# Moving a row store and a load behind the last shared V piece, and a new layout for the other branch's scratch

## The chip, the cores and the metric

The kernel runs on one core of a Trainium2 chip. The metric is the device time of one execution in microseconds (us); less is better. Times of single instructions come from one profiled execution.

## The reference

Two branches are computed from the same x and mixed by a gate. One is a recurrent attention over segments of 32 rows, in which 8 rows of each segment's output are carried to the next; the other is a gated feed-forward. S = 2048, Dm = 640, 32 heads of 192, Df = 1536.

```python
def _A_ref(x, mem0, Wq, Wk, Wv, Wo, seg_len):
    ...
    mem = mem0                                     # 8 rows
    for s in range(n_seg):                         # 64 segments
        xs = x[:, s * seg_len:(s + 1) * seg_len, :].copy()
        h = jnp.concatenate([mem, xs], axis=1)     # 40 rows
        q = jnp.einsum('btd,dhe->bhte', h, Wq)     # k and v alike
        ...
        p = _softmax(scores, axis=-1)
        o = jnp.einsum('bhqk,bhke->bhqe', p, v)
        o = jnp.einsum('bhte,hed->btd', o, Wo)
        mem = o[:, :M, :].copy()
        outs.append(o[:, M:, :])
...
g = _sigmoid((x * gate_w).sum(-1, keepdims=True))
a = _A_ref(x, A_mem0, A_Wq, A_Wk, A_Wv, A_Wo, A_seg_len)
b = _B_ref(x, B_w_gate, B_w_up, B_w_down)          # gelu(x wg) * (x wu), times w_down
return g * a + (1 - g) * b
```

## The kernel before

The program is one list of operations that a small scheduler of the kernel's own (`_Sched`) cuts into five streams, one for each engine. It does not reorder: within an engine the order is that in which the Python code adds them, and semaphores are put in where regions of memory overlap. A DMA is an operation of the engine that issues it. SP (SyncE) issues nearly all of them; in the first stage a few stand in the stream of ACT (ScalarE), since the variable `AUXQ` is "act" there and "sp" from line 909 on.

First stage, the feed-forward branch: four blocks of 512 rows. `ffn_gu` makes gate, up and their product, `ffn_down` the down projection in four steps of 128 rows. In each step PE (TensorE) writes two PSUM banks; ACT (L872) and then DVE (VectorE, L875) copy them to one of four row buffers (`brow`), and a DMA on ACT's queue (L878) stores the 128 rows to the scratch tensor `b_scr` in DRAM. A step's PSUM banks are used again two steps later, its row buffer a block later. Meanwhile SP loads attention weights that fit.

Second stage: 64 segments, one after the other, each written out as a list of items in `PROGS` (four lists, used in turn; segment s has list s % 4). An item ("g", n, k) is one step k = 0 to 4 of a group of projections; group 0 makes Q and K of the first eight heads' "octet", group 1 V of the first octet with Q and K of the second, group 6 V of the last octet. "tq", "tk", "sc", "ex", "pt", "pv" are transposes, scores, softmax and the product with V; ("wo", i, h) is the output projection. The wo items, the addition of the two partial sums and the transpose of the new memory rows (L1463) end a segment, and the next segment's first group needs those rows.

The weights do not all fit on the chip. Thirteen pieces of Q, K and V (384 KB each, one of them cut to 144 KB) and three of Wo (480 KB) share their place with a partner: the place holds the piece of the first octet or that of the last one. Even segments go through the octets upwards, odd ones downwards, so each place is swapped once in a segment: when a step has used the first octet's piece, `swap_loads` puts the load of its partner (L645, for the short one L642) on SP's queue, and it is needed later in the same segment. The five V pieces are swapped after the steps of group 1 and used in the steps of group 6; the K and Q pieces are swapped before them, those of Wo after ("wo", 0, 0) and ("wo", 0, 1).

Around them SP has small transfers, in the order of the code: `out_store` (L1015) writes the finished rows of the segment before from the buffer `bz` to the output; `x_load` (L751) fetches the next segment's rows into `xs`, from where POOL (GpSimd) copies them (`x_copy`, L799) when group 6 is done; `bz_load` (L1006) fetches the feed-forward rows of this segment into `bz`, after group 6, when the row store has landed; POOL scales them (L1042) and DVE mixes them with the attention rows (L1044). The carried rows of each four segments are mixed apart, with `bzl_load` (L1011) and `outl_store` (L1020). `bz` has 128 partitions: partition 32 j + t holds columns 160 j to 160 j + 159 of row t. Further loads and stores on SP bring projections of the left-over rows made ahead (`stg_load` L994, `left_store` L945, L950, `xl_load` L755).

In `segment`, the row store and the x load are added when item ("g", 1, 4) has been issued to PE, and the swap loads of that item, with the fifth V piece, behind them.

Of the kernel before, what the change touches and what calls it, by code (L numbers as in the profile page):

```python
# [6 lines left out]
BF = mybir.dt.bfloat16  # L7
# [224 lines left out]
def _build(nc, A_x, A_mem0, A_Wq, A_Wk, A_Wv, A_Wo, seg_len, w_gate, w_up, w_down,  # L232
           gate_w, out, opts=None):
    opts = dict(opts or {})
    Bsz, S, Dm = A_x.shape
# [3 lines left out]
    L = int(seg_len)  # L239
# [3 lines left out]
    DJ = Dm // 4  # L243
# [4 lines left out]
    NSEG = S // L  # L248
# [3 lines left out]
    XA = L - M  # L252
# [14 lines left out]
    S_ = _Sched(nc)  # L267
# [2 lines left out]

    x2 = A_x[0]
    out2 = out[0]
    b_scr = nc.dram_tensor("ffn_b_scratch", (S, Dm), BF, kind="Internal").ap()
    x_scr = nc.dram_tensor("x_scratch", (NSEG, 128, KT * XA), BF, kind="Internal").ap()
    xl_scr = nc.dram_tensor("left_x_scratch", (NG, 128, KT * 32), BF, kind="Internal").ap()
    g_scr = nc.dram_tensor("gate_scratch", (S,), F32, kind="Internal").ap()
# [431 lines left out]
    def rows(ap, g):  # L708
        v = ap[128 * g:128 * g + 128, :].rearrange("(s t) d -> s t d", t=L)
        return v[:, 0:XA, :], v[:, XA:L, :]  # L710
# [146 lines left out]
    def ffn_down(blk):  # L857
        n1 = min(Dm, 512)
        for a in range(FA):
            xb = 3 + 2 * (a % 2)  # L860
            yb = xb + 1
            fns = []
            for f in range(FT):
                fns.append(lambda e, f=f, a=a, xb=xb: e.matmul(ps[:, xb, 0:n1], hT_sb[:, f, a * 128:(a + 1) * 128], wd_sb[:, f, 0:n1],
                                                               start=(f == 0), stop=(f == FT - 1)))
                if Dm > 512:
                    fns.append(lambda e, f=f, a=a, yb=yb: e.matmul(ps[:, yb, 0:Dm - 512], hT_sb[:, f, a * 128:(a + 1) * 128], wd_sb[:, f, 512:Dm],
                                                                   start=(f == 0), stop=(f == FT - 1)))
            wr = [r_ps[xb]] + ([r_ps[yb]] if Dm > 512 else [])
            S_.add("pe", fns, reads=[r_wd] + r_hT, writes=wr, name="ffn down %d %d" % (blk, a))  # L870
            bs = a % NBR
            S_.add("act", lambda e, bs=bs, xb=xb: e.activation(out=brow[bs][:, 0:n1], in_=ps[:, xb, 0:n1], func=ACTF.Copy),  # L872
                   reads=[r_ps[xb]], writes=[r_brow[bs]], name="ffn b evac")
            if Dm > 512:
                S_.add("dve", lambda e, bs=bs, yb=yb: e.tensor_copy(out=brow[bs][:, 512:Dm], in_=ps[:, yb, 0:Dm - 512]),  # L875
                       reads=[r_ps[yb]], writes=[r_brow[bs]], name="ffn b evac2")
            row0 = blk * FB + a * 128
            S_.add(AUXQ, lambda e, bs=bs, row0=row0: e.dma_start(b_scr[row0:row0 + 128, :], brow[bs]),  # L878
                   reads=[r_brow[bs]], writes=[Rg("dr", row0, row0 + 128)], dma_sem="bw%d" % bs, watch=True,
                   name="b store %d" % row0)  # L880

    ffn_transposes(0)
    x_stage(0)
# [119 lines left out]
               name="Kl s%d i%d" % (s, i))  # L1003

    def bz_load(s):
        S_.add(AUXQ, lambda e: e.dma_start(bz, b_scr[L * s:L * s + L, :].rearrange("t (j n) -> j t n", j=4)),  # L1006
               reads=[Rg("dr", 128 * (s // 4), 128 * (s // 4) + 128)], writes=[r_bz], dma_sem="bz", name="bz load s%d" % s)

    def bzl_load(g):
        for j in range(4):  # L1010
            S_.add(AUXQ, lambda e, j=j: e.dma_start(bzl[32 * j:32 * j + 32], rows(b_scr, g)[1][:, :, DJ * j:DJ * (j + 1)]),  # L1011
                   reads=[Rg("dr", 128 * g, 128 * g + 128)], writes=[r_bzlj[j]], dma_sem="bzl%d" % j, name="bzl load g%d" % g)

    def out_store(s):
# [360 lines left out]
    def segment(s):  # L1375
        g, q = s // 4, s % 4
        n_wo, nqkv = n_wos[q], nqkvs[q]
        held = []
        post = []
        for n, item in enumerate(PROGS[q]):  # L1380
            kind, i = item[0], item[1]
            if kind == "g":
                if item[1:] == (0, 0):
                    left_fill(s, 0)
                    if s:
                        S_.add("pool", lambda e: e.memset(pl_sb[0:104, :, M * ((q + 3) % 4):M * ((q + 3) % 4) + M], 0.0),
                               writes=[r_p], name="pl zero s%d" % s)
                proj(s, item)
                ki = [j for m, j in GROUPS[i] if m == 1 and item[2] == KT - 1]
                kind, i = ("k", ki[0]) if ki else ("", 0)  # L1390
                if kind == "k" and i == 1:
                    if s > 0:
                        out_store(s - 1)
                    if s + 1 < NSEG:
                        x_load(s + 1)
            elif kind == "tq":
                row_transp(s, 0, i)
            elif kind == "tk":
                row_transp(s, 1, i)
            elif kind == "sc":  # L1400
                scores(s, i)
                if i == 0 and q == 0 and g > 0:
                    left_sums(g - 1)
            elif kind == "ex":
                softmax(s, i)
            elif kind == "pt":
                p_transp(s, i)
            elif kind == "pv":
                pv_oct(s, i)
                if i == 0 and q == 3 and g + 1 < NG:  # L1410
                    xl_load(g + 1, XLx, r_XLx, "xlx")
            elif kind == "lf":
                if i == q and unit(s, item[2]):
                    if item[3] == 0:
                        for m in range(2):
                            lb[item[2], m] = misc_bank(s)
                    for m in range(2):
                        LBK[m] = lb[item[2], m]
                    left_mm(*unit(s, item[2]), item[3], unit_piece)
            elif kind == "vb":  # L1420
                if q == 3 and g + 1 < NG:
                    if i == 0:
                        lb["v"] = misc_bank(s)
                    vl_mm(s + 1, i)
            elif kind == "le":
                if i == q and unit(s, item[2]):
                    if n > n_wo:
                        post.append(item[2:] + (n,))
                    else:
                        left_evac(s, *item[2:], n)  # L1430
            else:
                held = wo_part(s, item)
                if i == 2 and item[2] == 0 and q == 0 and g > 0:
                    outl_store(g - 1)
                if q == 3 and item != last_wo:
                    wo_left(s, held)
            if item == gate_at[q]:
                gate_now(s)
            swap_loads(s, item)
            if item == ("wo", 2, 1) and s + 1 < NSEG:  # L1440
                stg_load(s + 1, 0)
            if s == 0 and item == ("g", 0, KT - 1):
                load_residents(3, lambda key: key[0] < 3 and on_tmp(key))
            if s == 0 and item == late_at:
                load_residents(3, lambda key: key[0] == 3)
            if n == nqkv:
                bz_load(s)
                if q == 2:
                    bzl_load(g)
                if q == 3 and g + 2 < NG:  # L1450
                    xl_load(g + 2, XL, r_XL, "xl0")
            if n == nqkv and s + 1 < NSEG:
                x_copy(s + 1)
            if n == nqkv and q == 3:
                scale_left(g)
        kv = [x.rearrange("p (c k) -> p c k", k=KT) for x in (Zt, ps[:, OB2, SC:512], zsum)]
        for i in range(2):
            ka, kb = KA[i], KA[i + 1]
            S_.add("dve", lambda e, ka=ka, kb=kb: e.tensor_tensor(
                out=kv[0][:, :, ka:kb], in0=kv[1][:, :, ka:kb], in1=kv[2][:, :, ka:kb], op=ALU.add),  # L1460
                reads=[r_ps[OB2], r_zp], writes=[r_Z[i]] + ([r_PT] if i == 0 else []), name="Z%s evac s%d" % ("a" if i == 0 else "", s))
            if s + 1 < NSEG:
                S_.add("dve", lambda e, ka=ka, kb=kb: e.transpose(  # L1463
                    out=XB4[:, :, ka:kb, XA:L].rearrange("p g k i -> p k g i"), in_=kv[0][:, :, ka:kb].rearrange("p c k -> p k c")),
                    reads=[r_Z[i]], writes=[r_Hm[i], r_Qm, r_Ql], name="Tm%d s%d" % (i, s))
        mix(s)
        if "v" in lb:
            vl_evac(s + 1, octet(s + 1, 0), lb.pop("v"), "act")
        for i in post:
            left_evac(s, *i)  # L1470
        if q == 3:
            wo_left(s, held)
            if s + 1 == NSEG:
                left_sums(g)
        if s + 1 < NSEG:
            stg_load(s + 1, 1)
# [84 lines left out]
```

## Time and profile before

| | us |
|---|---|
| time, median of 3 runs | 1728.7 (1721.29 to 1739.44) |
| the profiled execution | 1730.04 |
| its span on the core | 1728.2 |
| busy: PE / PEld / DVE / ACT / POOL | 1595.5 / 830.6 / 961.2 / 798.0 / 413.9 |
| first stage, about | 185 |
| DMA: HBM read / written | 458.64 MB / 21.11 MB |

PE is the matrix engine's matmuls, PEld its weight loads. "Lnnn" is a line of the kernel. A row of the timeline has the start in us from the span's start, the length, the engine and the instruction; SPq and ACTq are issues of DMAs, which take issue time on that engine's queue and land later. In square brackets stands the idle time of the engine ahead of the row and what ended it. A row of the view of waits has who waited for whom, the total in us, the number of waits and the longest.

### The profile page before, as it was taken

How to read it: one execution, taken by the hardware profiler on the slowest of the kernel's cores; microseconds unless marked ns; L12 is line 12 of the kernel's file. 1: busy time of each engine (PE TensorE's matmuls, PEld its weight loads, DVE VectorE, ACT ScalarE, POOL GpSimd, SP SyncE). 2: the span in 40 equal slices, each digit the busy share in tenths (PEclk: the TensorE clock that was granted, in tenths of full speed). 3: DMA queues.
4: the chain of work that ended last, by engine and by line, in shares of the span. 5: the costliest groups of instructions: out<-in, count | busy, mean ns of one | idle time of the engine just before them, and what ended most of it. 6: DMA issues, size and time to landing. Idle time of an engine off the chain costs nothing. (4 is left out here: it accounts for less than half of the span.)

```text
span 1728.2 us, 80542 instructions
## 1 busy us (share of the span) xinstructions
PE 1595.5 (92%) x39162; PEld 830.6 (48%) x31501; DVE 961.2 (56%) x2939; ACT 798.0 (46%) x1899; POOL 413.9 (24%) x1098
## 2 busy tenths in 40 slices
PE   9999899999898999999998999999898999999887
PEld 4554345444544545444554545454445445454444
DVE  2222655656565565656565656656555655556554
ACT  3222444444444454545454454545444544445444
POOL 1100122222222222222222222222222222222222
PEclk9999999999999999999999999999999999999999
DMA  9914888878888788888888888888878877879876
GB/s 317 322 54 136 305 288 303 289 259 287 302 285 272 280 301 307 294 285 290 286 301 295 279 293 294 300 307 297 282 265 294 303 283 279 296 283 318 276 272 246
DMA packets 273761, 485.00 MB, mean 281 GB/s; under 512 B 107624, under 2 KB 142720, under 8 KB 273408
## 3 DMA queue, kind: packets, MB, share of 16 engines
q1 hardware_dynamic: 270424, 476.80, 78.8%
q8 instruction: 276, 4.52, 1.0%
q10 hardware_dynamic: 2984, 3.05, 0.5%
q14 instruction: 77, 0.63, 0.1%
HBM read 458.64 MB, written 21.11 MB: 278 GB/s over the span
## 5 line engine op out<-in xcount | busy, mean ns | idle before, releaser
L1115 PE MATMUL ps<-arena 128*32 128x384 bf16 x9940 | 719.5, 328 | 40.5 <-DVE arena L1463 12.0
L226 PE MATMUL ps<-arena 128*32 128x384 bf16 x7680 | 584.3, 326 | 9.3 <-DVE arena L1284 3.5
L1115 PEld LDWEIGHTS ps<-arena 128*32 128x32 bf16 x9940 | 257.9, 96 | 421.4 <-issue 269.1
L1149 DVE STREAM_TRANSPOSE arena<-arena 128x384 bf16<-128x384 bf16 x512 | 275.2, 560 | 116.2 <-ACT arena L1135 115.9
L1135 ACT ACTIVATE arena<-ps 128x384 bf16<-128x384 f32 x512 | 237.0, 490 | 181.0 <-PE ps L1115 155.9
L1275 PE MATMUL ps<-arena 128*32 128x320 bf16 x6144 | 283.5, 302 | 11.5 <-issue 11.4
L1265 POOL COPY arena<-arena 128x96 bf16<-128x96 bf16 x256 | 163.3, 638 | 480.1 <-ACT arena L1257 431.9
L1257 ACT ACTIVATE arena<-ps 128x480 bf16<-128x480 f32 (+1 forms) x256 | 137.3, 537 | 183.2 <-PE ps L1248 180.0
L1275 PEld LDWEIGHTS ps<-arena 128*32 128x32 bf16 x6144 | 174.8, 107 | 63.9 <-issue 18.0
L1000 POOL COPY arena<-arena 128x96 bf16<-128x96 bf16 x256 | 69.4, 271 | 502.6 <-PE ps L1169 402.3
L1138 ACT ACTIVATE arena<-ps 128x384 bf16<-128x384 f32 x256 | 125.0, 488 | 125.0 <-PE ps L1115 122.7
L1181 DVE TENSOR_REDUCE arena<-ps 104x4 f32<-104x160 f32 x256 | 82.9, 324 | 167.0 <-PE ps L1169 165.5
L1231 ACT ACTIVATE arena<-ps 128x448 bf16<-128x448 f32 x192 | 104.7, 545 | 72.1 <-PE ps L1218 72.1
L1246 PE MATMUL ps<-arena 128*64 128x160 bf16 x1536 | 119.6, 243 | 16.3 <-ACT arena L1138 11.8
L1195 DVE TENSOR_REDUCE arena<-ps 104x4 f32<-104x160 f32 x256 | 81.1, 317 | 95.6 <-ACT ps L1193 93.5
L1246 PEld LDWEIGHTS ps<-arena 128*64 128x64 bf16 x1536 | 79.9, 109 | 85.6 <-ACT arena L1231 27.3
L1193 ACT ACTIVATE ps<-ps 104x160 f32<-104x160 f32 x256 | 74.3, 290 | 96.9 <-DVE ps L1183 95.5
L931 PE MATMUL ps<-arena 128*32 128x384 bf16 x1280 | 108.4, 327 | 1.9 <-issue 1.7
L1248 PE MATMUL ps<-arena 128*64 128x64 bf16 x1536 | 103.3, 193 | 3.0 <-issue 3.0
L938 DVE STREAM_TRANSPOSE arena<-arena 128x384 bf16<-128x384 bf16 x128 | 73.8, 576 | 55.4 <-ACT arena L936 49.7
L1183 DVE TENSOR_TENSOR ps<-ps,arena 104x160 f32<-104x160 f32 x256 | 85.1, 332 | 8.8
L1298 PE MATMUL ps<-arena 128*32 128x160 bf16 x3072 | 73.4, 233 | 17.4 <-ACT arena L1033 9.1
(84 smaller groups left out, 1813.5 us busy)
## 6 DMA issues: line engine op xcount, KB each, us to landing
arena<-in_A_Wk_dram SPq DMA_DIRECT2D x335, 384.0 KB, 6.6
arena<-in_A_Wv_dram SPq DMA_DIRECT2D x335, 384.0 KB, 8.4
arena<-in_A_Wo_dram SPq DMA_DIRECT2D x205, 480.0 KB, 6.0
arena<-in_A_Wq_dram SPq DMA_DIRECT2D x146, 384.0 KB, 5.7
arena<-left_qk_scratch SPq DMA_DIRECT2D x126, 96.0 KB, 2.4
left_qk_scratch<-arena SPq DMA_DIRECT2D x49, 192.0 KB, 3.5
arena<-in_A_Wq_dram SPq DMA_DIRECT2D x63, 144.0 KB, 3.7
left_qk_scratch<-arena SPq DMA_DIRECT2D x30, 96.0 KB, 3.0
```

The lines of the kernel that those rows point to most:

```text
L226: return e.add_instruction(mybir.InstMatmult(name=nm, start_tensor_calc=like["start"], stop_tensor_calc=stop, tile_size=(128, 32), tile_po ...
L931: fns.append(lambda e, outp=outp, rhs=rhs, j=j: e.matmul(outp, lhs, rhs, start=(k == 0), stop=(k == KT - 1), tile_position=(0, 32 * j)))
L1115: fns.append(lambda e, outp=outp, rhs=rhs, j=j: e.matmul(outp, lhs, rhs, start=(k == 0), stop=(k == KT - 1), tile_position=(0, 32 * j)))
L1135: S_.add("act", lambda e, m=m, bk=bk: e.activation(out=rows_sb[m], in_=ps[:, bk, 0:384], func=ACTF.Copy), reads=[r_ps[bk]], writes=[r_rows ...
L1138: S_.add("act", lambda e, i=i, bk=bk: e.activation(out=v_sb[i % NVB].rearrange("p (c n) -> p c n", c=3), in_=ps[:, bk, 0:384].rearrange("p ...
L1149: S_.add("dve", lambda e: e.transpose(out=dst[:, :, 0:L], in_=rows_sb[m].rearrange("p (c r) -> p c r", r=L)), reads=[r_rows[m]], writes=[r ...
L1231: S_.add("act", lambda e: e.activation(out=PT, in_=ps[:, bank, 0:PTW + 128], func=ACTF.Copy), reads=[r_ps[bank]], writes=[r_PT], name="pT ...
L1246: return [lambda e: e.matmul(full, v[:, e0:e0 + 64], PTm[:, i], start=True, stop=False, tile_position=(0, 64 * i), skip_group_check=True), ...
L1248: lambda e: e.matmul(part, vl[:, e0:e0 + 64], PTl[:, i], start=False, stop=True, tile_position=(0, 64 * i), skip_group_check=True)]
L1257: S_.add("act", lambda e: e.activation(out=apx(u[:, 0, 0, :], [[R, na], [3 * R, 4], [1, R]]), in_=ps[:, A, 0:na * W].rearrange("p (c t r) ...
L1265: S_.add("pool", lambda e: e.tensor_copy(out=uTl[:, q, :, 12 * oc:12 * oc + 12].rearrange("p i (t c) -> p t c i", c=3), in_=u[:, :, :, L:R ...
L1275: fns.append(lambda e, i=i, t=t, j=j, gv=gv: e.matmul(ps[32 * j:32 * j + 32, bank, 0:2 * DJ].rearrange("p (h n) -> p h n", h=2), lhs2[i], ...
```

## The change

Two edits. In `segment`, a flag is set at item ("g", 1, 4), and the row store and the x load are added behind `swap_loads` of that item instead of ahead of it, so that the load of the fifth V piece comes first. And the scratch `b_scr` gets the shape (segment, quarter of the columns, row, 160 columns): the 128 rows of a store are four segments, so each store becomes four DMAs of 32 rows with a semaphore of its own, and the load of `bz` reads one contiguous block. The left-over load reads its 8 rows of four segments from the new shape.

```diff
-    b_scr = nc.dram_tensor("ffn_b_scratch", (S, Dm), BF, kind="Internal").ap()
+    b_scr = nc.dram_tensor("ffn_b_scratch", (NSEG, 4, L, DJ), BF, kind="Internal").ap()
@@ ffn_down
-            S_.add(AUXQ, lambda e, bs=bs, row0=row0: e.dma_start(b_scr[row0:row0 + 128, :], brow[bs]),
-                   reads=[r_brow[bs]], writes=[Rg("dr", row0, row0 + 128)], dma_sem="bw%d" % bs, watch=True,
-                   name="b store %d" % row0)
+            for i in range(4):
+                S_.add(AUXQ, lambda e, bs=bs, row0=row0, i=i: e.dma_start(
+                    b_scr[row0 // L + i].rearrange("j t n -> t j n"), brow[bs][L * i:L * i + L].rearrange("t (j n) -> t j n", j=4)),
+                    reads=[r_brow[bs]], writes=[Rg("dr", row0 + L * i, row0 + L * i + L)], dma_sem="bw%d%d" % (bs, i), watch=True,
+                    name="b store %d" % row0)
@@ bz_load
-        S_.add(AUXQ, lambda e: e.dma_start(bz, b_scr[L * s:L * s + L, :].rearrange("t (j n) -> j t n", j=4)),
+        S_.add(AUXQ, lambda e: e.dma_start(bz, b_scr[s].rearrange("j t n -> (j t) n")),
@@ bzl_load
-            S_.add(AUXQ, lambda e, j=j: e.dma_start(bzl[32 * j:32 * j + 32], rows(b_scr, g)[1][:, :, DJ * j:DJ * (j + 1)]),
+            S_.add(AUXQ, lambda e, j=j: e.dma_start(bzl[32 * j:32 * j + 32], b_scr[4 * g:4 * g + 4, j, XA:L, :]),
@@ segment
+        turn = False
         for n, item in enumerate(PROGS[q]):
...
                 if kind == "k" and i == 1:
-                    if s > 0:
-                        out_store(s - 1)
-                    if s + 1 < NSEG:
-                        x_load(s + 1)
+                    turn = True
...
             swap_loads(s, item)
+            if turn:
+                if s > 0:
+                    out_store(s - 1)
+                if s + 1 < NSEG:
+                    x_load(s + 1)
+                turn = False
```

## Prediction, made before the changed kernel was run

> **What bounds the kernel now.** I read the page's busy lines first, then the windows by stage, then who waited for whom, and last the timeline of SP (SyncE, which issues nearly all DMAs) in one segment.
>
> ```profile
> span 1728.2 us, 80542 instructions
> PE 1595.5 (92%) x39162; PEld 830.6 (48%) x31501; DVE 961.2 (56%) x2939; ACT 798.0 (46%) x1899; POOL 413.9 (24%) x1098
> ...
> q10 hardware_dynamic: 2984, 3.05, 0.5%
> ```
>
> The windows by stage have the length, the busy time of PE, PEld, DVE, ACT and POOL with counts, the clock, the DMA engines' share and GB/s. The first two rows are the feed-forward branch, the third is the 64 segments.
>
> ```profile
> 0.00:90.00 90.00, 86.39 (x537) 43.64 (x547) 23.17 (x40) 24.90 (x39) 11.40 (x30) 1.00 0.94 313
> 90.00:185.00 95.00, 91.25 (x748) 43.36 (x634) 29.09 (x62) 26.92 (x47) 5.85 (x16) 0.99 0.38 117
> 185.00:1728.00 1543.00, 1417.89 (x37886) 743.61 (x30328) 908.95 (x2837) 746.16 (x1813) 396.61 (x1052) 1.00 0.82 289
> ```
>
> TensorE is busy 1417.9 of 1543 us of the segments, at full clock: a segment is 1543/64 = 24.1 us long, of which PE idles 1.95 us. The DMA engines are busy 82% of that stage. Two things can set the end here: PE's own work, and the stream of weight pieces that are swapped in each segment. From the view of waits I take the rows of PE and PEld that name a DMA, and one of POOL (total us, times, longest):
>
> ```profile
> PEld ps L1115 <- DMA arena<-in_A_Wv_dram: 15.4, 30, 2.2
> ...
> PE ps L1115 <- DMA arena<-in_A_Wk_dram: 11.1, 22, 2.0
> ...
> PEld ps L1298 <- DMA arena<-in_A_Wo_dram: 8.1, 15, 1.0
> POOL arena L1042 <- DMA arena<-ffn_b_scratch: 7.5, 15, 1.4
> PE ps L1115 <- DMA arena<-in_A_Wv_dram: 6.4, 10, 1.7
> ...
> PE ps L1298 <- DMA arena<-in_A_Wo_dram: 4.9, 12, 0.8
> ```
>
> PE stands still for V pieces 6.4 us, for Wo pieces 4.9 us and for K pieces 11.1 us in the whole run. The PEld rows (weight loads, partly under running matmuls) are the upper ends. K pieces are requested and land before anything that is moved, so theirs stay. That leaves 6.4 us at stake for V, at the most 15.4.
>
> **The move of the row store and the x load.** This is SP in one segment of the second program (start, length of the issue):
>
> ```profile
> 796.69 1.63 SPq L645 DMA_DIRECT2D arena<-in_A_Wv_dram  x3
> 798.36 0.56 SPq L1015 DMA_DIRECT2D out_dram<-arena  x1
> 798.96 0.60 SPq L751 DMA_DIRECT2D arena<-x_scratch  x1
> 799.61 0.51 SPq L645 DMA_DIRECT2D arena<-in_A_Wv_dram  x1
> 803.86 1.28 SPq L645 DMA_DIRECT2D arena<-in_A_Wo_dram  x3
> 805.66 0.55 SPq L1006 DMA_DIRECT2D arena<-ffn_b_scratch  x1
> 810.79 0.37 SPq L945 DMA_DIRECT2D left_qk_scratch<-arena  x1
> ```
>
> The fifth shared V piece (k = 4; V4 below) is issued at 799.61, 0.05 us after the x load's issue ends: SP doesn't wait for PE there, so V4 simply moves up to 798.36, by 1.25 us. The row store (L1015) moves back by V4's 0.51 and the x load likewise. What they were moved past is V4 alone; nothing else on SP is between.
>
> Whether V4 also lands 1.25 us earlier, the landings of V2, V3, V4 and of the x load tell (each answer is for that one issue: start in us, and us from it to landing):
>
> ```profile
> L645 SPq DMA_DIRECT2D arena<-in_A_Wv_dram x1: 562/562/562, 797.3 to 797.3; - x1
> ...
> DMA to landing us min/median/max: 8.2/8.2/8.2
> ```
>
> ```profile
> L645 SPq DMA_DIRECT2D arena<-in_A_Wv_dram x1: 442/442/442, 797.9 to 797.9; - x1
> ...
> DMA to landing us min/median/max: 8.5/8.5/8.5
> ```
>
> ```profile
> L645 SPq DMA_DIRECT2D arena<-in_A_Wv_dram x1: 512/512/512, 799.6 to 799.6; - x1
> ...
> DMA to landing us min/median/max: 7.9/7.9/7.9
> ```
>
> ```profile
> L751 SPq DMA_DIRECT2D arena<-x_scratch x1: 602/602/602, 799.0 to 799.0; - x1
> ...
> DMA to landing us min/median/max: 7.6/7.6/7.6
> ```
>
> V2 lands at 805.5, V3 at 806.4, the x load at 806.6, V4 at 807.5. V3 follows V2 by 0.9 us and V4 follows V3 by 1.1: the transfers stand in a queue that takes each about 8 us, and the two small ones between them cost 0.2 us of it. So V4 lands 0.2 us earlier, not 1.25 (ends: 0, if another transfer sets its last share, and 1.25, if the issue did); I take 0.2, from the spacing. Does PE wait for V4? The timeline of PE and POOL around it:
>
> ```profile
> 807.55 0.22 PE L1213 MATMUL ps<-arena 104*32 104x80 bf16 x4 [0.30 <-DVE arena L1199]
> ...
> 807.72 0.34 PE L1115 MATMUL ps<-arena 128*32 128x384 bf16 x4
> ...
> 808.14 0.29 POOL L799 COPY arena<-arena 128x120 bf16<-128x120 bf16 x1 [0.36 <-PE ps L1115]
> ...
> 811.65 0.39 PE L1298 MATMUL ps<-arena 128*32 128x160 bf16 x12 [0.74 <-DMA arena<-in_A_Wo_dram]
> ```
>
> V4's matmuls run at 807.72, and PE's idle 0.30 us ahead of them was ended by DVE (the softmax), not by V4, which had landed at 807.5. An earlier V4 brings nothing in this segment. The ten PE waits for V are shared by five pieces, of which V4 comes last and with most time. I put the gain at 0.5 us: ten waits, one in four for V4, 0.2 us each. Ends: 0 and 6.4 us. The last Wo piece is what PE waits for at 811.65; ahead of it in the queue stand the same bytes as before, in another order, so its 0.74 us stay.
>
> What comes later: the x load lands behind V4, so at about 807.5 instead of 806.6. Its reader, POOL's copy L799, starts at 808.14 and was released by PE, which had finished V4; 0.6 us of slack are left, and behind that PE's next segment starts only after 811.65. Without that cover it would cost at most the 0.9 us per segment by which the x load is later. I take 0.
>
> The row store lands later too, and SP's next load of bz (L1006) waits for it. The view of waits of SP:
>
> ```profile
> SPq L1006 <- DMA out_dram<-arena: 10.5, 15, 2.1
> ```
>
> In the segment shown, L1006 is issued at 805.66 and could slip to 807.5 at most. Queued behind it on SP is the store at 810.79, which waits for DVE; from 806.21 on SP has 4.6 us free. So the 1.8 us vanish in it: 0 (if the cover were gone: first rival on the slow side, below).
>
> **The new scratch layout.** The load of bz reads one contiguous 40 KB block instead of four strided ones; its 128 runs of 320 B stay. It may be issued 0.1 us faster and land earlier; who gains is POOL L1042 (7.5 us of waits), then the mix on DVE. No PE row names either, so 0; the left-over loads (L1011) keep their form. The stores of the feed-forward branch change more: 16 DMAs of 128 rows of 1280 B become 64 of 32 rows of 4 x 320 B, on ACT's queue. The timeline of ACT in that stage, and issue times of stores by form (ns min/median/max):
>
> ```profile
> 120.94 0.60 ACT L872 ACTIVATE arena<-ps 128x512 bf16<-128x512 f32 x1 [1.49 <-PE ps L867]
> 121.97 0.35 ACTq L878 DMA_DIRECT2D ffn_b_scratch<-arena  x1
> 124.20 0.60 ACT L872 ACTIVATE arena<-ps 128x512 bf16<-128x512 f32 x1 [2.66 <-PE ps L867]
> ...
> 133.96 0.60 ACT L852 ACTIVATE arena<-ps 128x512 bf16<-128x512 f32 x1 [1.31 <-PE ps L846]
> ```
>
> ```profile
> L878 ACTq DMA_DIRECT2D ffn_b_scratch<-arena x16: 326/349/353, 40.8 to 171.7; - x16
> ```
>
> ```profile
> L945 SPq DMA_DIRECT2D left_qk_scratch<-arena x49: 372/380/1337, 175.3 to 1578.3; - x49
> ```
>
> ```profile
> L1020 ACTq DMA_DIRECT2D out_dram<-arena x2: 728/740/753, 1724.8 to 1725.6; - x2
> ```
>
> One step of 128 rows takes 124.20 - 120.94 = 3.26 us. ACT uses 0.60 for its copy, 0.43 waiting for DVE's, 0.35 for the store: 1.38. Three more stores at 0.38 (L945, the nearest form: four runs from each partition) are 1.14 more: 2.52 of 3.26, under PE's matmuls. At 0.74 (L1020, the dearest store that ACT issues) the step takes 0.60 + 0.43 + 2.96 = 3.99, 0.73 too long, 16 times: 11.7 us if all of it shows. Lower end 0. After the fourth step of a block the next thing on ACT is the gelu, which has 1.31 us idle ahead of it, more than 1.14. After the last block ACT's first copy of the left-over rows starts up to 1.1 us late, and a DVE chain behind it holds PE once:
>
> ```profile
> PE ps L226 <- DVE ps L786: 2.2, 1, 2.2
> ```
>
> That wait can grow by 0 to 1.1 us; ACT's idle time between those copies takes most of it, so +0.3. Bytes stay the same; queue q10 gets 48 x 128 = 6144 packets more, all small.
>
> The Trainium skill speaks against this part: "DMA: Bandwidth & Descriptors", Specifications, wants at least 512 B per transfer for full rate, since shorter ones are read, changed and written back. By it the stores of 320 B would cost about twice; as an estimate from that page's rule that is q10's 0.5% of the span again, some 9 us of DMA time, half of it in the first 90 us, where the engines are busy 94%. No run here shows it yet for stores of this size beside larger ones, and the sum goes without it.
>
> **The sum.** The profiled execution took 1730.0 us (span 1728.2 and 1.8 around it): 1730.0 - 0.5 + 0.3 = 1729.8. It lies 1.3 above the median of the three runs, 1728.7, so on that scale I predict 1728.5.
>
> **Rivals.**
> (a) The stream is relieved more than I think: with the row store off V4's way and the bz load no longer strided, transfers stop lagging and PE's waits for V and Wo go, both in PEld rows, 15.4 + 8.1 = 23.5 us: 1705. For it: these waits come in a stage whose DMA engines are 82% busy. Against: V2 and V3 are ahead of the moved transfers, and the bytes ahead of Wo are the same. The Trainium skill, "DMA: Bandwidth & Descriptors", Why a DMA increments its semaphore by 16, has a rule that bears on it: a DMA uses as many of the 16 engines as divide its slowest dimension, so bz's four strided blocks would sit on 4 engines and the contiguous load on 16; no row here tells the engines apart.
> (b) Slower: the row store's later landing holds SP at L1006 past its cover, and the K requests of the next segment, in order behind it, go out late. Programs 1 and 3, where L1006 follows the row store most closely, are 32 segments; at 1.1 us each (V4's spacing) that is 35 us: 1764. For it: 15 such waits exist already. Against: 4.6 us of idle SP behind it. It decides once the delay exceeds those 4.6 us.
> (c) ACT becomes the bound in the down projection, at 0.74 us a store: 1728.5 + 11.7 = 1740. For it: that row is ACT's own. Against: it is a store of 8 rows in four blocks, another form.
> (d) V4 can't be issued earlier since PE has not released its slot: then the order on SP changes and V4's landing doesn't: 1729. Against: the zero wait at 799.61.
>
> **How the numbers follow.** My forecast 0.78, (a) 0.06, (b) 0.06, (c) 0.07, (d) 0.03. A measurement of this kernel can tell about 1%, 17 us, from no change. (a) is faster by more, (b) slower by more, the rest within: 0.06, 0.88, 0.06. The range: 1728.5 less the 6.4 us of V and some of the runs' own spread (1721 to 1739) gives 1719; plus (c) 1740. It leaves out (a) and (b).
>
> **What would show it.** Right: in the profile after, SP's L751 and L1015 stand behind the fifth V load; V4's landing moves by some tenths of a us; the PE waits for Wv stay between 4 and 7 us and PE's busy time stays; the ACT stores take under 0.45 us each and the first two windows keep their PE time. Wrong: Wv and Wo waits of PE near zero (a), longer waits of L1006 together with more Wk waits (b), PE idle in the down projection (c).

## The result and the profile after

The changed kernel takes 1733.95 us (median of 22 runs, 1725.45 to 1744.3), the kernel before 1725.88 in the runs beside it (22 runs, 1718.03 to 1739.44): ratio 1.0047, 95% interval 1.0032 to 1.0062. It is 8 us slower. The profiled execution took 1733.92 us.

The page of the changed kernel, and its windows by stage (columns as before):

```profile
span 1732.2 us, 80614 instructions
...
PE 1602.0 (92%) x39162; PEld 833.9 (48%) x31501; DVE 962.1 (56%) x2939; ACT 798.5 (46%) x1899; POOL 415.8 (24%) x1098
...
q10 hardware_dynamic: 9896, 3.05, 0.8%
```

```profile
0.00:90.00 90.00, 86.18 (x536) 43.28 (x546) 23.07 (x40) 24.81 (x39) 11.44 (x30) 1.00 0.95 312
90.00:185.00 95.00, 89.93 (x724) 42.75 (x612) 28.97 (x62) 27.05 (x47) 5.88 (x16) 1.00 0.41 118
185.00:1732.00 1547.00, 1425.84 (x37912) 747.87 (x30344) 910.08 (x2837) 746.61 (x1813) 398.51 (x1052) 0.99 0.82 288
```

The first stage is as long as before (its last copy at L872 starts at 170.9 us, at 170.8 in before); what is lost is lost in the segments, with PE 7.9 us longer busy at a granted clock of 0.99 instead of 1.00. The waits of PE for weight pieces (total us, times, longest), then two waits of other engines:

```profile
PE ps L1117 <- DMA arena<-in_A_Wk_dram: 11.5, 21, 1.5
...
PE ps L1300 <- DMA arena<-in_A_Wo_dram: 3.9, 10, 0.8
...
PE ps L1117 <- DMA arena<-in_A_Wv_dram: 2.7, 9, 0.6
PE ps L226 <- DMA arena<-in_A_Wq_dram: 2.5, 3, 1.4
```

```profile
SPq L1008 <- DMA out_dram<-arena: 31.3, 25, 2.6
...
POOL arena L1044 <- DMA arena<-ffn_b_scratch: 9.9, 15, 1.0
```

V waits fell from 6.4 to 2.7 us. New is a row for Wq, 2.5 us where the view of before has 0.2. The wait of the bz load for the row store grew from 10.5 to 31.3 us. The issues of the two lines that changed their form (ns min/median/max), the bz load before and after, then the store after:

```profile
L1006 SPq DMA_DIRECT2D arena<-ffn_b_scratch x64: 537/548/632, 200.5 to 1714.4; - x64
```

```profile
L1008 SPq DMA_DIRECT2D arena<-ffn_b_scratch x64: 326/431/1842, 200.6 to 1718.0; - x64
```

```profile
L879 ACTq DMA_DIRECT2D ffn_b_scratch<-arena x64: 309/453/1570, 40.5 to 173.5; - x64
```

The bz load's median is 0.12 us shorter, but some issues take over three times as long as before. What follows one of them on SP, in the changed kernel, at the end of a segment with s % 4 = 2 ("program 2" from here; start and length in us):

```profile
727.74 1.84 SPq L1008 DMA_DIRECT2D arena<-ffn_b_scratch  x1
729.63 2.92 SPq L1013 DMA_DIRECT2D arena<-ffn_b_scratch  x4
732.59 0.44 SPq L952 DMA_DIRECT2D left_qk_scratch<-arena  x1
733.14 1.48 SPq L996 DMA_DIRECT2D arena<-left_qk_scratch  x1
734.67 0.43 SPq L645 DMA_DIRECT2D arena<-in_A_Wk_dram  x1
735.14 0.43 SPq L642 DMA_DIRECT2D arena<-in_A_Wq_dram  x1
```

The same place in the kernel before, in another segment of that program:

```profile
1117.79 0.56 SPq L1006 DMA_DIRECT2D arena<-ffn_b_scratch  x1
1118.39 2.59 SPq L1011 DMA_DIRECT2D arena<-ffn_b_scratch  x4
1121.03 0.45 SPq L950 DMA_DIRECT2D left_qk_scratch<-arena  x1
1121.58 0.45 SPq L994 DMA_DIRECT2D arena<-left_qk_scratch  x1
1122.07 0.44 SPq L645 DMA_DIRECT2D arena<-in_A_Wk_dram  x1
```

SP has no idle time between the bz load and the next segment's first K piece: every row begins 0.04 to 0.11 us after the end of the one ahead. So what the bz load takes longer, K is requested later. The two rows of DVE that end these segments and the next ones, after and before:

```profile
730.82 0.29 DVE L1469 STREAM_TRANSPOSE arena<-arena 128x96 bf16<-128x96 bf16 x1
...
758.08 0.30 DVE L1469 STREAM_TRANSPOSE arena<-arena 128x96 bf16<-128x96 bf16 x1
```

```profile
1120.91 0.29 DVE L1463 STREAM_TRANSPOSE arena<-arena 128x96 bf16<-128x96 bf16 x1
...
1145.31 0.30 DVE L1463 STREAM_TRANSPOSE arena<-arena 128x96 bf16<-128x96 bf16 x1
```

In before K is requested 0.87 us after the segment's start and the segment takes 24.4 us; after the long issue it is 3.56 us (the stage load L996, with 1.48, has its part in it) and 27.3 us. PE in that long segment (in brackets the idle time ahead and what ended it), and the windows around the last of the waits:

```profile
741.42 0.33 PE L226 MATMUL ps<-arena 128*32 128x384 bf16 x4 [0.88 <-DMA arena<-in_A_Wq_dram]
...
743.35 0.35 PE L1117 MATMUL ps<-arena 128*32 128x384 bf16 x4 [0.59 <-DMA arena<-in_A_Wk_dram]
745.01 0.35 PE L1117 MATMUL ps<-arena 128*32 128x384 bf16 x4 [1.32 <-DMA arena<-in_A_Wk_dram]
...
745.94 0.49 PE L1117 MATMUL ps<-arena 128*32 128x384 bf16 x4 [0.16 <-DMA arena<-in_A_Wk_dram]
```

```profile
742.00:745.80 3.80, 1.87 (x46) 0.99 (x42) 1.91 (x7) 1.00 (x3) 0.54 (x2) 1.00 1.03 399
745.90:749.40 3.50, 3.46 (x66) 2.23 (x70) 0.78 (x2) 1.53 (x3) 0.64 (x1) 0.52 1.04 373
749.60:753.00 3.40, 3.40 (x100) 2.68 (x96) 1.19 (x5) 0.76 (x2) 0.65 (x1) 1.00 0.95 347
```

PE waits 2.95 us for Q and K pieces, and then a second price comes: for 3.5 us the granted clock is 0.52, so that 3.5 x 0.48 = 1.7 us more are lost. Such stretches at half clock are what brings the stage's mean from 1.00 to 0.99: seven begin in this trace between the first segment and the last, two in that of before. But only two of the seven, and one of the two, begin in a segment that follows program 2, so this pair of traces alone doesn't tie the clock to the bz load.

### The profile page after: what moved, and what is told of

Read it like the earlier page. It is cut to its first block, busy times and chain, and to the rows that moved or that the text cites. A ratio compares the mean times of both kernels' runs of the same rounds, so it can differ in the third digit from the quotient of the medians.

```text
span 1732.2 us, 80614 instructions
## 1 busy us (share of the span) xinstructions
PE 1602.0 (92%) x39162; PEld 833.9 (48%) x31501; DVE 962.1 (56%) x2939; ACT 798.5 (46%) x1899; POOL 415.8 (24%) x1098
## 4 chain that ended last, share of the span: by engine, by line
PE 72%; DMA 13%; DVE 7%; ACT 3%; issue 3%; ACTq 1%; SPq 0%; POOLq 0%; DVEq 0%; POOL 0%
PE ps L1117 21%; PE ps L226 15%; PE ps L1277 10%; DMA arena<-in_A_Wk_dram 7%; PE ps L1248 4%; DMA arena<-in_A_Wo_dram 3%; PE ps L1300 3%; PE ps L849 3%; PE ps L846 3%; PE ps L1171 2%; DMA arena<-in_A_Wv_dram 2%; PE ps L933 2%; PE ps L1158 2%; PE ps L864 2%; PE ps L1166 1%
```

## The experiments

Each ratio is to the kernel before, run beside it, with its 95% interval in brackets. "128-row form" is the bz load from 128 equal rows, as in the changed kernel; "four-block form" is that of before, four blocks of 32 rows that can't be joined.

**First: which part.** e1 has the order change alone, e2 the new layout alone, e3 the layout with a padding row that brings the four-block form back:

```diff
# e3
-    b_scr = nc.dram_tensor("ffn_b_scratch", (NSEG, 4, L, DJ), BF, kind="Internal").ap()
+    b_scr = nc.dram_tensor("ffn_b_scratch", (NSEG, 4, L + 1, DJ), BF, kind="Internal").ap()[:, :, 0:L, :]
-        ... e.dma_start(bz, b_scr[s].rearrange("j t n -> (j t) n"))
+        ... e.dma_start(bz, b_scr[s])
```

> Only the order changes: the row store and the x load behind the fifth V piece; scratch layout as before. Theory M (the move costs the time): SP's load of bz waits longer for the row store (31 us of such waits in the changed kernel, 10.5 before), and the requests behind it go out late: ratio about 1.005, waits of that load for the row store near 30 us. Theory L (the layout costs it): ratio 1.000 within 0.002, although the waits for the row store grow all the same.

Measured: 1728.65 against 1728.06 us, 1.0006 (0.9979 to 1.0034). The move costs nothing that can be measured, though the bz load's wait for the row store is 26.0 us there.

> Only the scratch layout changes; order as before. Theory L: the contiguous load of bz, issued ahead of the left-over loads and the first K requests of the next segment, holds SP longer (mean 0.73 us against 0.56 in the segments with left-over loads), and the K and Q pieces of the segment after go out 0.3 to 0.5 us late: ratio about 1.005, segments of the fourth program 0.3 to 0.4 us longer. Theory M: 1.000 within 0.002.

Measured: 1732.64, 1.0039 (1.0011 to 1.0067). The layout has the loss.

> The layout alone, but each quarter padded by one row, so that the load of bz is four separate blocks again (as before) and not one contiguous one; the stores stay four to a step. Theory L with the load of bz as its cause: 1.000 within 0.002, the issue of that load at 0.55 us again. Theory L with the stores of the first stage as its cause: as the layout alone. Theory M: 1.000.

Measured: 1728.61, 1.0009 (0.9986 to 1.0032). With the same 64 stores and the same bytes the loss is gone; apart from the padding row, only the form of the bz load is other than in e2.

**Second: the form of the load, or the length of SP's queue.** e4 is the changed kernel with e3's padding. e5 adds two loads of 128 x 32 B behind the bz load of e2, e6 the same two in four-block form to e3, and e7 pads each row of e2 to 384 B:

```diff
# e5, behind bz_load(s); e6 with b_scr[s][:, :, 0:16]
+                for x_ in range(2):
+                    S_.add(AUXQ, lambda e, x_=x_: e.dma_start(bview(w_cap - 64 + 32 * x_, 32),
+                           b_scr[s].rearrange("j t n -> (j t) n")[:, 0:16]), ...)
# e7
+    b_scr = nc.dram_tensor("ffn_b_scratch", (NSEG, 4, L, DJ + 32), BF, kind="Internal").ap()[:, :, :, 0:DJ]
```

> The changed kernel with one difference: each quarter of the scratch is padded by one row, so that the load of bz is four blocks again and not one contiguous block. If the contiguous form of that load is the whole cost: ratio to the kernel before 1.001, at most 1.003. If the move and the layout cost only together, or the stores do: 1.004 to 1.006 as the changed kernel.

Measured: 1727.69 against 1725.68, 1.0011 (0.9993 to 1.0028).

> The layout alone (contiguous load of bz), with two more small loads behind each load of bz: 128 runs of 32 B each, contiguous form like that load. They carry nothing that is used. Theory S (a DMA over all partitions in this form costs the later transfers something, each time): the cost of the layout three times, ratio about 1.012. Theory Q (the issue time on SP costs): two more issues of 0.45 us, ratio about 1.01, and the same in the twin run. Theory B (something of the load of bz itself, its landing or the mix behind it): 1.004, no more than the layout alone.

Measured: 1748.93, 1.0133 (1.0106 to 1.016).

> The twin: padded layout (load of bz in four blocks), with two more small loads behind each load of bz, 128 runs of 32 B each, in the form of four blocks. They carry nothing that is used. Theory S: 1.001, as without them. Theory Q: two more issues of 0.55 us, ratio about 1.01 or a little over the other. Theory B: 1.001.

Measured: 1743.3, 1.0099 (1.007 to 1.0128).

> The layout alone, each row padded from 320 to 384 B, so that the load of bz has 128 equal rows in one dimension as in the changed kernel, but is no contiguous block. If the form of one dimension of 128 rows costs the time: 1.004, as the layout alone. If contiguous addresses in DRAM cost it: 1.000 to 1.001.

Measured: 1732.13, 1.0037 (1.0016 to 1.0058).

e7 shows that a contiguous block isn't the point: rows with holes between them cost the same as long as there are 128 equal ones. e6 was missed by two of the three theories: two small four-block loads, which transfer 8 KB, cost some 15 us (1.0099 against e3's 1.0009). Of the three, only a theory in which SP's issue time counts expects that. And the time is not lost evenly. By the DVE rows that end a segment, the mean segment that follows program 2 took 24.8 us in before, 25.0 in e2 and 25.3 in e3, but 26.6 in e5 and 26.5 in e6; in e5 and e6 the other three kinds were within 0.25 us of before. e5's waits of PE:

```profile
PE ps L1117 <- DMA arena<-in_A_Wk_dram: 21.0, 35, 1.8
...
PE ps L226 <- DMA arena<-in_A_Wq_dram: 6.7, 10, 1.2
```

So the next theory, P: only at the end of program 2 has SP no idle time ahead of K, and what counts is how long the bz load holds SP there. Its rival T: the load's spread over more DMA engines costs wherever it stands.

**Third: P against T by program.** e8 has the 128-row form in the other three programs and four blocks in program 2, e9 the reverse; the segments of program 2 read a second scratch, which takes a fifth store per 128 rows. e10 is the kernel before, e11 the changed one, with the bzl loads moved from the end of program 2 to a hole of SP in the next:

```diff
# e10, e11
                     xl_load(g + 1, XLx, r_XLx, "xlx")
+                if i == 0 and q == 3:
+                    bzl_load(g)
...
                 bz_load(s)
-                if q == 2:
-                    bzl_load(g)
# e8
-        ... e.dma_start(bz, b_scr[s].rearrange("j t n -> (j t) n"))
+        ... e.dma_start(bz, b2_scr[s] if s % 4 == 2 else b_scr[s].rearrange("j t n -> (j t) n"))
```

> Layout only, with the load of bz in two forms: 128 equal rows in the segments with s%4 of 0, 1 and 3, four separate blocks of 32 rows in those with s%4==2, which read a second padded scratch (one more store of 32 rows per 128 on ACT in the first stage). Theory P: only in the program s%4==2 does SP go from the load of bz to the next segment's first K piece without idle time (bz, four loads of bzl, a stage store, a stage load, then K, in before at 0.04 us each between them), and there the long issues of the 128-row form (1.0 to 1.8 us in 4 or 5 of 16) delay K; elsewhere SP idles 0.9 us or more afterwards. P expects no cost here: 0.9995 to 1.0015. Theory T (each load spread over 16 DMA engines costs by itself, through the engines or by its later landing): three quarters of the layout's 0.0039, so 1.003.

Measured: 1734.77 against 1726.04, 1.0041 (1.0013 to 1.0069).

> The other way round: 128 equal rows only where s%4==2, four blocks in the other three programs; the same additional store. P expects the whole cost of the layout, 1.0025 to 1.004. T expects a quarter of it, 1.001.

Measured: 1748.65, 1.0134 (1.0104 to 1.0163).

> The kernel before with the four loads of bzl moved from the end of the program s%4==2 to the hole of SP in the program s%4==3, behind the xlx load at 10.2 us, where SP has 2.6 us without work. P: SP has 2.6 us less ahead of the first K piece of s%4==3, which is requested at 0.9 us of that segment in before and at 0.13 us in the others; up to 0.8 us in 16 segments, 13 us: 0.9925 to 0.998. T says nothing of it; if SP's queue there is not on the path, 1.000.

Measured: 1715.94, 0.994 (0.9916 to 0.9964): faster than both kernels.

> The changed kernel with the same move of the bzl loads. P: with SP idle ahead of K the long issues of the 128-row form are covered, so the time of e10 within 0.0015 (0.9925 to 0.9985). T: e10's ratio plus 0.004.

Measured: 1720.34, 0.9971 (0.9952 to 0.999). That is 0.0031 above e10: not within P's 0.0015, and nearer to T's 0.004.

e8 and e9 carry a load of their own. The first segment ended 9 us later than in before (228.7 and 230.3 against 219.8, on the trace's clock), since the fifth store holds ACT ahead of the gelu of the next block; e8's row:

```profile
PE ps L847 <- ACT arena L853: 4.9, 3, 2.8
```

They can be compared with each other, and there P has the sign (e9 is 14 us slower), T hasn't, though 14 us is more than P gives. e10 shows the tail of program 2 directly. SP at its end, e10 and then e11:

```profile
1115.30 0.56 SPq L1006 DMA_DIRECT2D arena<-ffn_b_scratch  x1
1117.67 0.37 SPq L950 DMA_DIRECT2D left_qk_scratch<-arena  x1
1118.14 0.45 SPq L994 DMA_DIRECT2D arena<-left_qk_scratch  x1
1118.83 0.33 SPq L645 DMA_DIRECT2D arena<-in_A_Wk_dram  x1
```

```profile
1114.33 1.51 SPq L1008 DMA_DIRECT2D arena<-ffn_b_scratch  x1
1116.74 0.37 SPq L952 DMA_DIRECT2D left_qk_scratch<-arena  x1
1117.21 0.45 SPq L996 DMA_DIRECT2D arena<-left_qk_scratch  x1
1117.90 0.33 SPq L645 DMA_DIRECT2D arena<-in_A_Wk_dram  x1
```

In e11 an issue of 1.51 us is followed by 0.9 us of idle SP, and K goes out as it would have done anyway. PE's waits for K in e10:

```profile
PE ps L1115 <- DMA arena<-in_A_Wk_dram: 2.9, 6, 1.2
```

**Fourth: the bz load alone ahead of idle time.** e12 (before) and e13 (layout alone) issue the bz load of program 2 twelve steps sooner, where SP has 3.4 us to spare. e14 is e4 with the bzl loads moved.

```diff
# e12, e13
-            if n == nqkv:
+            if n == (nqkv - 12 if q == 2 else nqkv):
                 bz_load(s)
+            if n == nqkv:
```

> The kernel before with the load of bz in the program s%4==2 alone requested 12 steps sooner, between Wo's three requests and the left store, where SP has 3.4 us without work; nothing else is moved. P (SP's tail of s%4==2 sets the request of the next K piece, 0.9 us late in before): one request of 0.56 us less in the tail, 16 times: 9 us, 0.995 (0.993 to 0.998). If the tail is not on the path: 1.000.

Measured: 1716.94 against 1725.38, 0.9959 (0.9933 to 0.9985).

> The layout alone (128 equal rows) with the same earlier load in s%4==2. P: its long issues now fall ahead of SP's idle time and cost nothing: the ratio of e12 within 0.0015 (0.9935 to 0.9985). T (the 128-row form costs wherever it stands): e12's ratio plus 0.003 to 0.004.

Measured: 1721.38, 0.9967 (0.9948 to 0.9986): e12's ratio within 0.0008, as P said. It tests the cover less than it seems: at the earlier place only 2 of the 16 issues took over 0.65 us, against 5 of 16 in e2.

> The changed kernel with the padded scratch (four blocks) and the loads of bzl moved into s%4==3. It stands between the kernel before with that move, 0.994, and the changed kernel with it, 0.9971. P: the form of the load no longer matters there, all three are the same within the spread, 0.994 to 0.997. T: the padding takes the difference away: 0.994, and the 0.003 between those two is the form's price.

Measured: 1720.25, 0.9981 (0.9956 to 1.0006), outside what either theory gave. Four blocks did not bring e11 down to e10, so nothing here says that the form is what stands between those two.

**Fifth.** e15 is the kernel before with both moves, e16 the layout alone with the bzl loads moved.

> The kernel before with both moves: bz earlier in s%4==2, the loads of bzl in s%4==3. P: the tail of s%4==2 has 3.2 us less on SP, but the first K piece can come no sooner than 0.13 us into the segment, which the bzl move alone reaches in the median (mean 0.34): 0.2 us in 16 segments more than that, 0.992 (0.990 to 0.995). If the two gains added up: 0.990.

Measured: 1719.4 against 1726.35, 0.9964 (0.9947 to 0.9981). The gains don't add up, but the ratio is also above what P gave, and not below e10.

> The layout alone with the loads of bzl in s%4==3, between the kernel before with that move (0.994) and the changed kernel with it (0.9971). P: the form is free once SP has idle time there, and what is left of the 0.003 is the moved row store or scatter: 0.993 to 0.9955. T: the form is the 0.003: 0.9965 to 0.998.

Measured: 1723.26, 0.9984 (0.9967 to 1.0001), nearer to T's numbers than to P's. The seven kernels with SP relieved scatter from 0.994 to 0.9984: the mean of the four with four blocks (e10, e12, e14, e15) is 0.9961, that of the three with 128 rows (e11, e13, e16) 0.9974. These runs can't tell 0.0013 from nothing.

**Last: e8 and e9 without their confound.** The fifth store goes on SP's queue.

```diff
-            S_.add(AUXQ, lambda e, bs=bs, row0=row0: e.dma_start(
+            S_.add("sp", lambda e, bs=bs, row0=row0: e.dma_start(
                 b2_scr[row0 // L + 2].rearrange("j t n -> t j n"), ...
```

> e8 again, with the additional store of the first stage on SP instead of ACT, which in e8 and e9 made the first stage 9 to 10 us longer: 128 equal rows in s%4 of 0, 1 and 3, four blocks in s%4==2. P: no cost, 0.9995 to 1.0015, provided that the first stage ends near 219 us again. T: three quarters of the layout's 0.0039, 1.003.

Measured: 1725.0 against 1721.19, 1.0011 (0.9986 to 1.0035). The first segment ended at 221.1.

> e9 again in the same way: 128 equal rows in s%4==2 alone. P: the whole cost of the layout, 1.003 to 1.007 (e9 stood 0.009 above e8). T: a quarter of it, 1.001.

Measured: 1731.43, 1.0048 (1.0019 to 1.0077). The first segment ended at 220.4. Sixteen loads in the 128-row form cost as much as all 64 do; the other 48 cost nothing that can be measured. The waits of PE in e17 and in e18:

```profile
PE ps L1122 <- DMA arena<-in_A_Wk_dram: 7.0, 17, 1.3
...
PE ps L226 <- DMA arena<-in_A_Wq_dram: 0.6, 2, 0.3
```

```profile
PE ps L1122 <- DMA arena<-in_A_Wk_dram: 11.7, 24, 1.3
...
PE ps L226 <- DMA arena<-in_A_Wq_dram: 5.1, 6, 3.1
```

**All traces together.** Single executions of one kernel differ by over 1%, so rows were counted over the traces of all kernels. In the table, "K late" is the time from the end of a segment of program 2 to the next K request, and "next segment" the length of the segment that follows, both as means over 15 places in each trace, by the rows of SP and the DVE rows that end a segment. The waits are those of PE for K and Q pieces in a whole trace. The last column counts the stretches at half clock that begin in these next segments.

| kernels | K late, us | next segment, us | waits for K and Q, us | half clock |
|---|---|---|---|---|
| SP relieved: e10 to e16 | 0.38 | 24.53 | 3.2 | 0 |
| four blocks in program 2: before, e1, e3, e4, e8, e17 | 1.05 | 25.17 | 8.4 | 2.2 |
| 128 rows in program 2: after, e2, e7, e9, e18 | 1.30 | 25.43 | 14.0 | 3.8 |
| two more loads: e5, e6 | 2.40 | 26.53 | 24.5 | 9 |

The next segment is longer by what K is late, almost one to one: 0.98 us for each us, on a straight line fitted to the means of all 20 kernels. Long issues show the same inside the kernels. In the third row's kernels the bz issue of program 2 took over 0.65 us in 27 of 75 cases; the segment after a long one took 26.3 us, after a short one 24.9. In the relieved kernels with 128 rows (e11, e13, e16) 13 such issues were as long, and their next segments took 24.4 against 24.7 us. In the other programs of after, e2, e7, e8 and e17 long issues left the next segment as it was: 30 in program 0 (23.5 against 23.4 us), 14 in program 1 (22.8 against 23.0), 14 in program 3 (24.4 against 24.6).

How much of the loss this accounts for is less certain. The ratios of after, e2, e7 and e18 say 6 to 8 us. Between the second row and the third, 0.26 us in each of 16 segments is 4 us; 5.6 us more of waits and 1.6 more stretches at 1.7 us would be 8. And single traces scatter: that of e2 shows neither K later (0.99 us) nor longer waits (8.0 us), in an execution of 1728.7 us, below e2's median of 1732.6.

## Why the prediction was wrong

I forecast no change (1728.5, in a range of 1719 to 1740 that holds the measured 1733.95). The kernel is measurably slower, by 0.47%: less than the 1% that I took for the bound of the measurement. The mechanism was not among the four rivals: (b) had the path, a bz load that holds up the K requests behind it on SP, but with another cause and in other programs.

- **The step that failed** is "No PE row names either, so 0" for the bz load. I asked who waits for the load's data, not what stands behind it on SP. The price is the time that its issue holds SP ahead of K, and the term that I put at 0 is 6 to 8 us by the ratios. "It may be issued 0.1 us faster" was right of the median (0.43 against 0.55) and wrong of the tail: in the changed kernel 5 of 16 issues in program 2 take 1.0 to 1.8 us.
- **The second one** is "K pieces are requested and land before anything that is moved, so theirs stay". They come behind the bz load of the segment before. K's waits were the largest for weights in the profile of before, and with Q's they are the ones that grew, from 8.4 to 14.0 us on the mean.
- **Where it came from**: I read SP in one segment of program 1, found 4.6 us idle behind the bz load, and took that for all four programs. In program 2 four bzl loads, a store and a stage load fill that time.
- **The V piece**: right in the main. It is issued before the row store, 1.2 us closer to V3 than before, but lands only 0.1 us closer (median 0.94 us behind V3 against 1.02), so the order of the transfers counts, as argued, and not the issue. The time does not show it: e1 is at 1.0006. PE's waits for V were 2.7 us, not 4 to 7, but that can't be put down to the move: in the traces without it they go from 1.4 to 6.4 us.
- **Rival (b)**: the wait that it names grew, to 31.3 us at the bz load instead of 10.5, but no single one is longer than 2.6 us, so none exceeds the 4.6 us of cover that it had to. e1 has 26.0 us of it and loses nothing. This wait stands in programs 1 and 3, where idle time follows, as argued.
- **The stores**: 0.453 us each (estimated 0.38), and 4 x 0.453 + 1.03 = 2.84 of a step's 3.26 us still fit: the first windows are nearly unchanged. The packets of q10 grew by 6912: the 6144 of the sum, and 16 of 4 B for each of the 48 additional DMAs. e8 shows how near rival (c) was, since a fifth store made the first stage 9 us longer. The Trainium skill's 512 B rule ("DMA: Bandwidth & Descriptors", Specifications) would have given some 9 us of DMA time as an estimate; q10 rose from 0.5% to 0.8% of 16 engines' span, by its packets from 9.4 to 13.5 us, and the first stage got no longer.
- **Rival (a)** cited the Trainium skill's rule for the number of DMA engines ("DMA: Bandwidth & Descriptors", Why a DMA increments its semaphore by 16). The trace agrees: a bz load has 5 semaphore updates in before and in e3, 16 in after. It brought no relief.

Not settled: why some issues of the 128-row form are long. Issues of other lines in the same run, from 230 us on, in groups (ns min/median/max):

```profile
L645 SPq DMA_DIRECT2D arena<-in_A_Wk_dram x305: 328/432/1980, 231.6 to 1683.6; - x153
```

```profile
L996 SPq DMA_DIRECT2D arena<-left_qk_scratch x123: 319/398/1756, 229.9 to 1696.9; - x123
```

```profile
L1013 SPq DMA_DIRECT2D arena<-ffn_b_scratch x63: 597/620/690, 251.0 to 1699.8; - x63
```

```profile
L1017 SPq DMA_DIRECT2D out_dram<-arena x61: 562/567/590, 239.2 to 1687.3; - x61
```

The plain loads of 128 rows have the short median and the long tail, these DMAs in four blocks have neither. An obvious guess is that a long issue waits behind transfers under way, but the traces of after, e2 and e7 don't bear it out: with two or three other DMAs under way, of those whose landing the trace shows, 26 of 75 bz issues were over 0.65 us, with four or more 21 of 114. The cause of the tail stays open. Open too is whether 0.001 of the form's price remains where SP is relieved.

## What to carry to other kernels

In this kernel a DMA had two prices: when its data land, and how long its issue holds the queue. Before a request is called free, look in every variant of the loop at what is queued behind it and whether the queue has idle time before the next request that the bounding engine needs. Where it had none here, moving small requests away paid: e10 gained 0.6% by moving four loads, e12 0.4% by moving one.

## What was not expected of the hardware

- Short waits cost twice. PE was busy 1.87 of 3.80 us ahead of 745.9, with no idle stretch over 1.4 us, and then got a granted clock of 0.52 for 3.5 us. The other traces say the same. All stretches at half clock in a trace begin whole multiples of 3.413 us apart, within 3 ns. With the segments of all 20 traces cut into windows in line with them, 83 of the 88 windows at full clock in which PE was busy under half the time were followed by such a stretch, 48 of 739 between half and three quarters, and none of 7998 above that. The Trainium skill ("TensorE: Matmul & The Clock Gate", Part 1: The HAM clock gate) gives a window of about 3.4 us and half the clock, which the rows bear out; its table names an idle window as the cause, where here a window that was half idle was enough.
- With the same bytes and rows, the issue of a DMA took 535 to 617 ns in the four-block form (e3) and 326 to 1842 in the 128-row form (the changed kernel).
